# Attention and mixture-of-experts kernel: two loads by halves, three small pieces of work in other slots

## The chip, the cores and the metric

One core of one Trainium2 chip. The metric is the device time of one execution in microseconds (us); lower is better. Engines are named PE (TensorE matmul), DVE (VectorE), ACT (ScalarE), POOL (GpSimd) and SP (SyncE); L789 is line 789 of the kernel. The changed kernel has three more lines near the top, so that L789 of the kernel before is L792 there, L839 is L842, and so on.

## The reference

Attention over keys and values that are averaged in groups of eight, then four dense experts, each weighted by its normalised probability:

```python
# q, k, v: (8 batches, 8 heads, 576 rows, 64); x: (4608, 512); w1: (4, 512, 1024); w2: (4, 1024, 512)
k_p = k.reshape(B, H, 72, 8, D).mean(axis=3)
v_p = v.reshape(B, H, 72, 8, D).mean(axis=3)
attn = softmax(scale * q @ k_p.T)
x = (attn @ v_p)            # back to (B*S, H*D)
p = domain_probs / domain_probs.sum(-1, keepdims=True)
for e in range(4):
    out += p[:, e:e+1] * (relu(x @ w1[e]) @ w2[e])
```

## The kernel before

TensorE is nearly always busy (98% of the span): while the experts of one batch are multiplied, pieces of the attention of the next batches are put into numbered slots between groups of matmuls. Of each batch 512 rows are handled as four token blocks; the 64 rows left over are the "small" ones, handled for two batches together. All loads below are issued by GpSimd, in program order. "Folding" is the averaging over eight rows, done by VectorE in three halving additions.

```python
def load_w2(e):                       # w2 of expert e: 1 MB; only expert 0's comes in halves
    n = 1 if e else 2
    for i in range(n):
        fcs = slice(i * FCH // n, (i + 1) * FCH // n)
        nc.gpsimd.dma_start(out=w2_bf[:, e, fcs], in_=...)

def folds(raw):                       # first two of the three folds
    return [lambda n=n: nc.vector.tensor_add(
        out=raw[:, :, 0:n, :], in0=raw[:, :, 0:n, :], in1=raw[:, :, n:2 * n, :]) for n in (4, 2)]

def context(b, r, c_ps=None):         # 8 matmuls into the bank `att`, then a division by VectorE
    ...
    divide(c_ps, x_tok)

def rem_queries(i):                   # transpose of the small queries, a DMA on SP's queue
    qTr = apool.tile(...)
    nc.sync.dma_start_transpose(out=qTr..., in_=q_rems.pop(i)...)

def rem_scores(i):                    # small scores: 16 matmuls that read qTr
    ...

# first_chunk(), from the third weight sums on (what comes before is cut)
    each(*weight_sums(1)[0:3])
    down_plain(0, 1, 0)               # token block 0 of expert 1; VectorE adds it
    fold_first, *fold_rest = values_folds(1)
    fold_first()
    scores_of_two(1, 2, 0)
    each(*fold_rest)
    load_wide(0, 0); load_q(2); load_wide(0, 1)      # batch 2's keys, queries
    load_wide(1, 0); load_wide(1, 1)                 # batch 2's values
    load_q_rem(0); load_q_rem(1)                     # small queries of batches 0 and 1
    load_wide(1, 2)
    down_plain(0, 1, 1); down_plain(0, 1, 2)
    context(1, 0)
    down_plain(0, 1, 3)
    ...

# slots of batch 2 (BUSY): rem = slots of small queries, scores, context, ...
    plans[BUSY] = dict(
        queries=0, keys=4, values=12, scores=((9, 2), (12, 1), (15, 1)), contexts=(16, 18, 19, 21),
        q=6, k=(5, 8, 11, 14), v=(13, 16, 19, 26), x=(24, 25, 25, 25), rem=(0, 6, 8, 14),
    )
```

The softmax here doesn't subtract the row's maximum and nothing guards it: scores larger than these inputs give would overflow.

Of the kernel before, what the change touches and what calls it, by code (L numbers as in the profile page):

```python
# [17 lines left out]
def kernel(  # L18
# [10 lines left out]
    nc = tc.nc  # L29

    B, H, S, D = q.shape
# [3 lines left out]
    POOL = 8  # L35
# [7 lines left out]
    BUSY = 2  # L43
# [77 lines left out]
        n = 2 if b == 0 else 1  # L121
        return [slice(i * H // n, (i + 1) * H // n) for i in range(n)]

    def load_whole(b, src, nm):

        room = wt_bf[:, 1:E].rearrange("p e s i d -> p (e s i d)")
        at = {"kraw": 0, "vraw": 1}[nm] * H * POOL * D
        raw = room[0:SP, at:at + H * POOL * D].rearrange("j (h r d) -> j h r d", h=H, r=POOL)
        nc.gpsimd.dma_start(out=raw, in_=src[b].rearrange("h (j r) d -> j h r d", r=POOL))
        raws[(nm, b)] = raw  # L130

    def load_first(src, nm, g):
# [60 lines left out]
    def load_q_rem(b):  # L193
        if b % 2 == 0:
            q_rems[b // 2] = qpool.tile([P, H, D], BF16, name="q_rem", bufs=2)
        lo = (b % 2) * REM
        nc.gpsimd.dma_start(
            out=q_rems[b // 2][lo:lo + REM],
            in_=q[b, :, NT:S, :].rearrange("h p d -> p h d"),
        )  # L200
# [10 lines left out]
                )  # L211

    def load_w2(e):
        n = 1 if e else 2
        for i in range(n):
            fcs = slice(i * FCH // n, (i + 1) * FCH // n)
            nc.gpsimd.dma_start(
                out=w2_bf[:, e, fcs], in_=moe_w2[e].rearrange("(fc p) d -> p fc d", p=P)[:, fcs]
            )
# [47 lines left out]



    def folds(raw):  # L270

        return [lambda n=n: nc.vector.tensor_add(
            out=raw[:, :, 0:n, :], in0=raw[:, :, 0:n, :], in1=raw[:, :, n:2 * n, :]) for n in (4, 2)]

    def fold_wide(what, part):
        raw, wide = ((raw_k, wide_k), (raw_v, wide_v))[what]
# [53 lines left out]
        for _ in range(n):  # L330
            nc.tensor.matmul(w_ps[:, 0:cols], lhsT=zeros[:, 0:P], rhs=zeros[:, 0:cols])

    def values_folds(b):
        raw = raw_v if b >= BUSY else raws[("vraw", b)]
        return (folds(raw) if b < BUSY else []) + [lambda: nc.vector.tensor_add(
            out=vps[b % 3][:, :, 0:D], in0=raw[:, :, 0, :], in1=raw[:, :, 1, :])]



# [526 lines left out]
    def first_chunk():  # L866


        def each(*pieces):
            for piece in pieces:  # L870
                piece()

        sums = {e: first_weight_sums(e) for e in range(E)}

        def both(e, step):
            for unit in (1, 0) if e == 3 else (0, 1):
                up_product(0, e, unit, step)

        each(*(lambda n=n: x_sum(0, n) for n in range(4)), *sums[0][0:3])
        norm_probs()  # L880
        up(0, 1, (0, 1))
        hidden_sums(0, 0, 0)
        hidden_sums(0, 0, 1)
        up(0, 1, (2, 3))
        each(*sums[1][0:3])
        up(0, 1, (4,), bank=units[0][1][:])
        each(sums[2][0], sums[2][1], sums[2][3], sums[2][2])
        up(0, 1, (5,), bank=chains[0])
        both(2, 0)
        up(0, 1, (6,), bank=chains[1])  # L890
        both(2, 1)
        up(0, 1, (7,), bank=chains[0])
        last_sum = weight_sums(0)
        each(sums[0][3], sums[1][3], *last_sum[0:2])
        both(2, 2)
        down(0, 0, 0)
        both(2, 3)
        hidden_sums(0, 0, 2)
        down(0, 0, 1)
        both(2, 4)  # L900
        hidden_sums(0, 0, 3)
        down(0, 0, 2)
        both(2, 5)
        each(*last_sum[2:])
        down(0, 0, 3)
        both(2, 6)
        each(*sums[3][0:2])
        both(3, 0)
        down(0, 0, 4)
        both(3, 1)  # L910
        each(sums[3][3], sums[3][2])
        fold_keys(1)
        down(0, 0, 5)
        both(3, 2)
        down(0, 0, 6)
        both(3, 3)
        queries_of_two(0, att[:, 0], nc.scalar.copy)
        both(3, 4)
        both(3, 5)
        keys(1, every)  # L920
        queries_of_two(2, chains[0][:], nc.vector.tensor_copy)
        both(3, 6)
        load_w2(3)
        scores_of_two(1, 0, 0)
        each(*weight_sums(1)[0:3])
        down_plain(0, 1, 0)
        fold_first, *fold_rest = values_folds(1)
        fold_first()
        scores_of_two(1, 2, 0)
        each(*fold_rest)  # L930
        load_wide(0, 0)
        load_q(2)
        load_wide(0, 1)
        load_wide(1, 0)
        load_wide(1, 1)
        load_q_rem(0)
        load_q_rem(1)
        load_wide(1, 2)
        down_plain(0, 1, 1)
        down_plain(0, 1, 2)  # L940
        context(1, 0)
        down_plain(0, 1, 3)
        context(1, 1)
        turn(1, 0)
        hidden_sums(0, 3, 0)
        down_plain(0, 2, 0)
        context(1, 2)
        turn(1, 1)
        hidden_sums(0, 3, 1)
        down_plain(0, 2, 1)  # L950
        context(1, 3)
        turn(1, 2)
        each(*weight_sums(3)[0:3])
        down_plain(0, 2, 2)
        turn(1, 3)
        each(*(lambda n=n: x_sum(1, n) for n in range(3)))

    def pieces_later():


        at, amid = {0: [lambda: x_sum(1, 3)]}, {}

        def put_amid(slot, piece):
            amid[slot] = piece

        def put(slot, *pieces):
            at.setdefault(slot, []).extend(pieces)

        usual = dict(
            queries=-8, keys=-9, values=-2, scores=((2, 2), (9, 2)), contexts=(11, 14, 18, 21),  # L970
            q=1, k=(-2, 0, 5, 9), v=(-2, 0, 5, 9), x=(22, 25, 25, 25), rem=(-3, 17, 24, 25),
        )
        plans = {b: usual for b in range(BUSY, B + 1)}
        plans[BUSY] = dict(
            queries=0, keys=4, values=12, scores=((9, 2), (12, 1), (15, 1)), contexts=(16, 18, 19, 21),
            q=6, k=(5, 8, 11, 14), v=(13, 16, 19, 26), x=(24, 25, 25, 25), rem=(0, 6, 8, 14),
        )
        plans[B] = dict(usual, x=(24, 24, 25, 25), rem=(-3, 17, 21, 22))
        plans[BUSY + 1] = dict(usual, keys=-8, values=4, v=(5, 8, 12, 16))

        for b, plan in plans.items():
            start = 7 * E * (b - BUSY)

            def put_each(what, pieces):
                for slot, piece in zip(plan[what], pieces, strict=True):
                    put(start + slot, piece)

            if b == BUSY:
                put(start + 1, lambda: fold_wide(0, 0))
                put(start + 4, lambda: fold_wide(0, 1))  # L990
                put(start + 5, lambda: load_q_rem(BUSY))
                put(start + 8, lambda: fold_wide(1, 0))
                put(start + 12, lambda: fold_wide(1, 1))
            if b < B:
                put(start + plan["queries"], lambda b=b: queries(b))
                put(start + plan["keys"], lambda b=b: fold_keys(b))
                put(start + plan["keys"] + (b > BUSY), lambda b=b: keys(b, every))
                put(start + plan["values"], *values_folds(b))
                pair = 0
                for slot, n in plan["scores"]:  # L1000
                    if n == 2:
                        put(start + slot, lambda b=b, pair=pair: scores_of_two(b, pair))
                        put_amid(start + slot + 1, lambda b=b, pair=pair: scores(b, pair, 1))
                    else:
                        put(start + slot, lambda b=b, pair=pair: scores(b, pair))
                    pair += n

                for r, slot in zip((2, 3, 0, 1), plan["contexts"]):
                    put(start + slot, lambda b=b, r=r: context(b, r))
                    put(start + slot + 1, lambda b=b, r=r: turn(b, r))  # L1010
            if b + 1 < B:
                put(start + plan["q"], lambda b=b: load_q(b + 1), lambda b=b: load_q_rem(b + 1))
                for what in range(2):
                    put_each("kv"[what], [lambda b=b, what=what, part=part: load_part(b + 1, what, part)
                                          for part in range(NR)])
            if b % 2 == 0:
                i = b // 2 - 1
                put_each("rem", [lambda i=i, do=do: do(i)
                                 for do in (rem_queries, rem_scores, rem_context, rem_turn)])
            put_each("x", [lambda b=b, n=n: x_sum(b, n) for n in range(4)])  # L1020
        return at, amid

    ENG = mybir.EngineType
    with tc.manual_schedule(
# [20 lines left out]
        load_whole(1, k, "kraw")  # L1045
        load_q(1)
        load_w2(1)
        load_whole(1, v, "vraw")
        load_w2(2)
        first_chunk()  # L1050

# [64 lines left out]
```

## Time and profile before

| | kernel before |
|---|---|
| time, 3 runs at hand when the prediction was made | 492.33 us median (491.58 to 493.75) |
| time, 6 runs in the rounds of the comparison | 491.55 us median (491.17 to 493.75) |
| span of the profiled execution | 489.8 us |
| PE / DVE / ACT / POOL busy | 98% / 77% / 62% / 24% |

With TensorE busy for 480.9 of the 489.8 us, only the 8.9 us in which it stands still, the ramp at either end among them, can be won. The prediction shows the lines of the holes that it counts on (A, B, C). Timelines give start us, duration, operation. First, the small scores. The fences below hold three views: SyncE's timeline (start us, duration, operation), the list of DMA issues (KB and us from issue to landing; none given for a transpose), and TensorE's timeline.

```profile
73.56 1.20 SPq L484 DMA_TRANSPOSE qTr<-q_rem  x1
```

```profile
qTr<-q_rem SPq DMA_TRANSPOSE x1, 4.8
```

```profile
78.91 0.41 PE L497 MATMUL att<-qTr,kpT 64*128 64x64 bf16 x16
```

The transposed small queries are issued at 73.56 and land 4.8 us later, near 78.4. TensorE wants them at 78.91. No wait is listed, so it is easy to pass over; but what separates this from a wait is 0.5 us.

Second, the end. VectorE's last addition, then SyncE's waits (us in total, times, longest), then the DMA view from 485.0 to 489.8 us (busy tenths in 40 slices, and the instruction queue q14: packets, MB, share):

```profile
484.60 0.48 DVE L839 SCALAR_TENSOR_TENSOR acc<-o_ps,p_all,acc 128x256 f32<-128x256 f32 x1 [0.39 <-PE o_ps L822]
```

```profile
SPq L1111 <- DMA out_dram<-acc: 2.7, 2, 2.0
```

### The profile page before, as it was taken

The numbers are of one execution on the slowest core, as the hardware profiler recorded it, in microseconds if no ns is written. First come the engines' busy times: TensorE is split into PE (matmuls) and PEld (weight loads), VectorE is DVE, ScalarE is ACT, GpSimd is POOL, SyncE is SP. The second block draws the span as 40 slices with busy tenths as digits, with TensorE's granted clock in tenths as the row PEclk, the third lists the DMA queues.
The fourth block names the chain that finished last, engine by engine and source line by source line (L and its number), as shares of the span: only waits on it lengthen the run. The fifth ranks groups of instructions, "written<-read, shape, count | busy, mean of one in ns | idle before, by whom it ended". The sixth has DMA issues, their size and how long they took to land.

```text
span 489.8 us, 11600 instructions
## 1 busy us (share of the span) xinstructions
PE 480.9 (98%) x4721; PEld 412.2 (84%) x4721; DVE 378.7 (77%) x761; ACT 304.7 (62%) x583; POOL 117.3 (24%) x116
## 2 busy tenths in 40 slices
PE   7999999999999999999999999999999999999995
PEld 4868478888888888888889889888888888888884
DVE  5789999789768976797679876997678766876673
ACT  5787446855676567656765667656755576556650
POOL 8420414242523154016311442111011101110110
PEclk9999999999999999999999999999999999999999
DMA  9999999985997389345955397312111110004003
GB/s 199 210 206 203 192 164 158 103 86 58 116 104 60 79 83 140 34 84 61 154 48 90 28 167 62 70 21 66 34 23 23 38 50 3 12 23 87 0 1 88
DMA packets 101845, 41.98 MB, mean 86 GB/s; under 512 B 73872, under 2 KB 100240, under 8 KB 101792
## 3 DMA queue, kind: packets, MB, share of 16 engines
q0 software_dynamic: 56960, 22.42, 41.0%
q1 hardware_dynamic: 43728, 17.77, 17.0%
q10 hardware_dynamic: 1104, 1.05, 0.6%
q8 instruction: 37, 0.61, 0.5%
q14 instruction: 16, 0.13, 0.1%
HBM read 45.69 MB, written 9.44 MB: 113 GB/s over the span
## 4 chain that ended last, share of the span: by engine, by line
PE 84%; DMA 9%; POOL 2%; DVE 2%; ACT 1%; issue 0%; POOLq 0%; DVEq 0%; ACTq 0%
PE unit L695 39%; PE o_ps L763 39%; DMA w_bf<-in_moe_w_dram 9%; PE o_ps L789 1%; PE att L460 1%; PE unit L822 1%; POOL wt_bf L141 1%; DVE acc L839 1%; PE att L385 1%; POOL w_bf L208 1%; PE unit L385 0%; DVE H L675 0%; PE att L514 0%; DVE x_tok L422 0%; PE att L497 0%
## 5 line engine op out<-in xcount | busy, mean ns | idle before, releaser
L839 DVE SCALAR_TENSOR_TENSOR acc<-o_ps,p_all,acc 128x256 f32<-128x256 f32 (+1 forms) x285 | 127.0, 486 | 51.3 <-PE o_ps L763 36.2
L763 PEld LDWEIGHTS <-H 128*128 128x128 bf16 x1320 | 129.1, 98 | 15.0
L695 PEld LDWEIGHTS <-w_bf 128*128 128x128 bf16 x1088 | 105.2, 98 | 13.0 <-issue 0.2
L675 DVE CUSTOM_DVE_ANT_0 H<-unit,partial 128x512 bf16<-128x512 f32 x128 | 87.4, 685 | 26.1 <-ACT partial L710 12.6
L763 PE MATMUL o_ps<-w_bf,H 128*128 128x256 bf16 x792 | 102.6, 273 | 0.0
L695 PE MATMUL unit<-xT,w_bf 128*128 128x256 bf16 x704 | 100.4, 273 | 0.0
L777 POOL TENSOR_TENSOR acc<-acc,addend 128x512 f32<-128x512 f32 x24 | 30.4, 1266 | 255.5 <-ACT addend L775 211.9
L710 ACT COPY partial<-unit 128x512 f32<-128x512 f32 x128 | 72.3, 592 | 30.0 <-PE unit L695 30.0
L695 PEld LDWEIGHTS <-wu_bf 128*128 128x128 bf16 x816 | 77.6, 98 | 11.7 <-issue 2.5
L695 PE MATMUL unit<-xs,wu_bf 128*128 128x256 bf16 x512 | 77.0, 273 | 0.0
L763 PE MATMUL o_ps<-wt_bf,H 128*128 128x256 bf16 x528 | 68.4, 273 | 0.0
L712 ACT ACTIVATE H<-unit 128x512 bf16<-128x512 f32 x66 | 39.9, 605 | 31.7 <-PE unit L695 31.7
L763 PEld LDWEIGHTS <-S 128*128 128x128 bf16 x528 | 51.7, 98 | 6.0
L716 ACT ACTIVATE H<-unit 128x512 bf16<-128x512 f32 x66 | 39.6, 602 | 26.1 <-PE unit L695 25.8
L708 ACT COPY unit<-unit 128x512 f32<-128x512 f32 x68 | 39.4, 582 | 22.9 <-PE unit L695 17.3
L695 PE MATMUL unit<-xs,w_bf 128*128 128x256 bf16 x256 | 38.4, 273 | 0.0
L837 ACT ACTIVATE acc<-o_ps,p_all 128x256 f32<-128x256 f32 x72 | 30.7, 485 | 9.5 <-PE o_ps L763 7.5
L695 PE MATMUL unit<-xT,wu_bf 128*128 128x256 bf16 x240 | 35.7, 272 | 0.0
L151 POOL DMA_DIRECT2D kraw<-in_k_dram x20 | 26.4, 1320 | 37.6 <-DMA kraw<-in_k_dram 37.6
L763 PE MATMUL o_ps<-wt_bf,S 128*128 128x256 bf16 x264 | 34.2, 273 | 0.0
L763 PE MATMUL o_ps<-w_bf,S 128*128 128x256 bf16 x264 | 34.2, 273 | 0.0
L151 POOL DMA_DIRECT2D vraw<-in_v_dram x20 | 29.0, 1452 | 19.1 <-DMA vraw<-in_v_dram 19.1
(157 smaller groups left out, 506.6 us busy)
## 6 DMA issues: line engine op xcount, KB each, us to landing
out_dram<-acc SPq DMA_DIRECT2D x32, 256.0 KB, 4.5
w_bf<-in_moe_w_dram POOLq DMA_DIRECT2D x6, 1024.0 KB, 18.2
q_sb<-in_q_dram POOLq DMA_DIRECT2D x7, 512.0 KB, 9.9
vraw<-in_v_dram POOLq DMA_DIRECT2D x22, 144.0 KB, 6.8
kraw<-in_k_dram POOLq DMA_DIRECT2D x21, 144.0 KB, 5.8
w_bf<-in_moe_w_dram POOLq DMA_DIRECT2D x3, 512.0 KB, 16.7
wt_bf<-in_k_dram POOLq DMA_DIRECT2D x4, 144.0 KB, 5.4
wt_bf<-in_v_dram POOLq DMA_DIRECT2D x4, 144.0 KB, 4.5
```

The source lines that it names most:

```text
L141: nc.gpsimd.dma_start(out=raw[half * PR:(half + 1) * PR, g].rearrange("j h r d -> j h (r d)"), in_=src[0, h:h + 2].rearrange("h (j r) d -> ...
L151: nc.gpsimd.dma_start(out=raw[:], in_=rows_of(src, b, 2 * part, 2 * part + 2), accum_op=ALU.add if part else ALU.bypass)
L675: nc.vector._custom_dve(TENSOR_ADD_SAT, out=dst, in0=ps, in1=part, s0=LARGEST, s1=0.0)
L695: nc.tensor.matmul(ps[:, n * HN:(n + 1) * HN], lhsT=lhs[:, kc, f:f + P], rhs=rhs[:, kc, :], start=(not grows and n == 0 and kc == 0), stop ...
L708: nc.scalar.copy(out=banks[1][:], in_=ps)
L710: nc.scalar.copy(out=part[:, step - 2], in_=ps)
L712: nc.scalar.activation(out=quarter(0, 0), in_=ps, func=ACT.Relu)
L716: nc.scalar.activation(out=quarter(0, 1), in_=ps, func=ACT.Relu)
L763: nc.tensor.matmul(ps[:, j], lhsT=lhs[:, i, j * P:(j + 1) * P], rhs=rhs[:, i, :], start=(not grows and i == 0 and j == 0), stop=(i == HF - 1),
L777: nc.gpsimd.tensor_add(out=dst, in0=dst, in1=addend[:])
L837: nc.scalar.activation(out=dst, in_=o_ps, func=ACT.Copy, scale=prob)
L839: nc.vector.scalar_tensor_tensor(out=dst, in0=o_ps, scalar=prob, in1=dst, op0=ALU.mult, op1=ALU.add,)
```

## The change

Its intent: let TensorE start on expert 2's w2 when half of it is there; let VectorE hand back a bank between the folds of batch 1's values instead of after them; bring the small queries forward, ahead of batch 2's values, with the small scores a slot later; and move a context so that its bank is free in time.

```diff
-    def load_whole(b, src, nm):
+    def load_whole(b, src, nm, n=1):
...
-        nc.gpsimd.dma_start(out=raw, in_=src[b].rearrange("h (j r) d -> j h r d", r=POOL))
+        for i in range(n):
+            hs = slice(i * H // n, (i + 1) * H // n)
+            nc.gpsimd.dma_start(
+                out=raw[:, hs], in_=src[b].rearrange("h (j r) d -> j h r d", r=POOL)[:, hs])
...
     def load_w2(e):
-        n = 1 if e else 2
+        n = 2 if e in (0, 2) else 1
...   (folds and values_folds take a slice of heads, hs)
-        each(*weight_sums(1)[0:3])
+        rest = weight_sums(1)[0:3]
+        each(*rest[0:2])
         down_plain(0, 1, 0)
-        fold_first, *fold_rest = values_folds(1)
+        lo, hi = slice(0, H // 2), slice(H // 2, H)
+        each(*values_folds(1, lo))
+        scores_of_two(1, 2, 0)
+        fold_first, *fold_rest = values_folds(1, hi)
         fold_first()
-        scores_of_two(1, 2, 0)
+        down_plain(0, 1, 1)
         each(*fold_rest)
         load_wide(0, 0)
         load_q(2)
         load_wide(0, 1)
+        load_q_rem(0)
+        load_q_rem(1)
         load_wide(1, 0)
         load_wide(1, 1)
-        load_q_rem(0)
-        load_q_rem(1)
         load_wide(1, 2)
-        down_plain(0, 1, 1)
         down_plain(0, 1, 2)
         context(1, 0)
+        rest[2]()
...
-            ... contexts=(16, 18, 19, 21),
-            ... rem=(0, 6, 8, 14),
+            ... contexts=(16, 17, 19, 21),
+            ... rem=(0, 7, 8, 14),
...
-        load_whole(1, v, "vraw")
+        load_whole(1, v, "vraw", 2)
```

More of the change, by code (lines that the diff above doesn't have):

```diff
@@ L266, in one_bank, with folds @@
         return spare_bank() if b == 0 else two_banks(b)[:, 0]
-    def folds(raw):
+    def folds(raw, hs=slice(0, H)):
         return [lambda n=n: nc.vector.tensor_add(
-            out=raw[:, :, 0:n, :], in0=raw[:, :, 0:n, :], in1=raw[:, :, n:2 * n, :]) for n in (4, 2)]
+            out=raw[:, hs, 0:n, :], in0=raw[:, hs, 0:n, :], in1=raw[:, hs, n:2 * n, :]) for n in (4, 2)]
     def fold_wide(what, part):
@@ L331, in idle, with values_folds @@
             nc.tensor.matmul(w_ps[:, 0:cols], lhsT=zeros[:, 0:P], rhs=zeros[:, 0:cols])
-    def values_folds(b):
+    def values_folds(b, hs=slice(0, H)):
         raw = raw_v if b >= BUSY else raws[("vraw", b)]
-        return (folds(raw) if b < BUSY else []) + [lambda: nc.vector.tensor_add(
-            out=vps[b % 3][:, :, 0:D], in0=raw[:, :, 0, :], in1=raw[:, :, 1, :])]
+        return (folds(raw, hs) if b < BUSY else []) + [lambda: nc.vector.tensor_add(
+            out=vps[b % 3][:, hs, 0:D], in0=raw[:, hs, 0, :], in1=raw[:, hs, 1, :])]
     def queries(b, pair=0):
@@ L974, in pieces_later @@
         plans[BUSY] = dict(
-            queries=0, keys=4, values=12, scores=((9, 2), (12, 1), (15, 1)), contexts=(16, 18, 19, 21),
-            q=6, k=(5, 8, 11, 14), v=(13, 16, 19, 26), x=(24, 25, 25, 25), rem=(0, 6, 8, 14),
+            queries=0, keys=4, values=12, scores=((9, 2), (12, 1), (15, 1)), contexts=(16, 17, 19, 21),
+            q=6, k=(5, 8, 11, 14), v=(13, 16, 19, 26), x=(24, 25, 25, 25), rem=(0, 7, 8, 14),
         )
```

## The prediction

> **What bounds the kernel now.** I read the page first (busy shares, then the slices), then a table of busy time by stretches, then TensorE's timeline around the one stretch that isn't full, then VectorE's timeline there, and last the chain that ended last.
>
> The page, part 1:
>
> ```profile
> PE 480.9 (98%) x4721; PEld 412.2 (84%) x4721; DVE 378.7 (77%) x761; ACT 304.7 (62%) x583; POOL 117.3 (24%) x116
> ```
>
> TensorE is busy for 480.9 of 489.8 us. Of the 8.9 us that it isn't, 3.1 lie in the first 20 us and 5.2 in the last 9.8 (from the table by stretches: 7.73 and 9.14 of 10 us, and 4.56 of 9.80), which the change doesn't touch. Between 60 and 480 us it is busy everywhere but for 0.07 us near 104. The stretch where the change works has this row (columns: stretch, length, busy us and instructions of each engine, clock, DMA share, GB/s):
>
> ```profile
> 55.00:60.00 5.00, 4.54 (x37) 2.41 (x36) 4.38 (x10) 0.53 (x1) 3.35 (x4) 1.00 1.18 181
> ```
>
> 0.46 us idle, then. TensorE's timeline in it:
>
> ```profile
> 53.09 3.63 PE L789 MATMUL o_ps<-w_bf,H 128*128 128x512 bf16 x16
> 56.55 0.42 PE L460 MATMUL att<-vp,expT 72*128 72x65 bf16 x8
> 57.07 1.89 PE L789 MATMUL o_ps<-w_bf,H 128*128 128x512 bf16 x8
> 58.79 0.42 PE L460 MATMUL att<-vp,expT 72*128 72x65 bf16 x8
> 59.05 0.39 PE L478 MATMUL unit<-ident,x_tok 128*128 128x128 bf16 x4
> 59.80 1.89 PE L789 MATMUL o_ps<-w_bf,partial 128*128 128x512 bf16 x8 [0.36 <-DMA w_bf<-in_moe_w_dram]
> ```
>
> Durations here carry a tail, so I count from start to start. Eight 512-column matmuls take 1.73 us (56.55 - 53.09 = 3.46 for sixteen), eight 65-column ones 0.26 (58.79 to 59.05), four transposes 0.22 (61.79 to 62.01 later on). Two holes appear. The context at 56.55 should give way at 56.81, but the next group starts at 57.07: hole A, 0.26 us, not listed as idle as the tail hides it. The transposes should end at 59.27, but the next group starts at 59.80: hole B, 0.53 us. B is put down to a transfer, and the chain says which:
>
> ```profile
> 28.85 30.91 DMA w_bf<-in_moe_w_dram
> 59.76 0.04 issue
> 59.80 0.38 PE o_ps L789
> ```
>
> It is expert 2's w2, issued at 28.85 and landed whole at 59.76. A is VectorE's; its timeline:
>
> ```profile
> 53.26 0.74 DVE L839 SCALAR_TENSOR_TENSOR acc<-o_ps,p_all,acc 128x512 f32<-128x512 f32 x1
> 53.95 1.95 DVE L272 TENSOR_TENSOR wt_bf<-wt_bf 72x2048 bf16<-72x2048 bf16 x2
> 55.93 0.42 DVE L335 TENSOR_TENSOR vp<-wt_bf 72x512 bf16<-72x512 bf16 x1
> 56.27 1.40 DVE L839 SCALAR_TENSOR_TENSOR acc<-o_ps,p_all,acc 128x512 f32<-128x512 f32 x2
> ```
>
> Token block 3 writes the bank of block 1, whose add stands behind all three folds of batch 1's values. That add runs from 56.27 to about 57.0, just ahead of 57.07.
>
> The third hole, C, is near 104: a context starts at 104.73 where the group ahead (103.62, 0.87 from start to start) ends at 104.49, so 0.24 us.
>
> ```profile
> 103.62 1.04 PE L763 MATMUL o_ps<-w_bf,S 128*128 128x256 bf16 x8
> 104.73 0.42 PE L460 MATMUL att<-vp,expT 72*128 72x65 bf16 x8
> ```
>
> All contexts of a batch share the bank `att`; the next must wait till VectorE has divided the one before (columns as above):
>
> ```profile
> 99.35 0.88 DVE L839 SCALAR_TENSOR_TENSOR acc<-o_ps,p_all,acc 128x256 f32<-128x256 f32 x2 [1.30 <-ACT H L712]
> 100.15 0.20 DVE L421 RECIPROCAL inv<-att 128x8 f32<-128x8 f32 x1
> 100.38 0.69 DVE L422 TENSOR_TENSOR x_tok<-att,inv 128x512 bf16<-128x512 f32 x1
> ...
> 103.98 0.69 DVE L422 TENSOR_TENSOR x_tok<-att,inv 128x512 bf16<-128x512 f32 x1
> ```
>
> The division of the slot 18 context ends at 104.67, which fits 104.73. So A + B + C = 1.03 us, 0.2% of the time, is all that this change can win.
>
> [...] a 512-column matmul is listed with a mean of 379 ns, while starts are 1.73/8 = 216 ns apart; this is what hides A. [...] Here the fold additions take 1218 ns for 2048 elements, 688 for 1024 and 424 for 512: 530 ns per 1024, and about 158 ns left over. [...] an addition of 256 elements should show about 290 ns.
>
> **The change part by part.**
>
> 1. w2 of expert 2 by halves. Expert 0's w2 has already been in halves: the chain has the transfer ahead of it, w1 of expert 2, landed at about 28.6 (13.15 + 15.40), and VectorE waited till 33.72 for the second half of expert 0's w2, which lies just behind. That is 5.1 us for 1024 KB, so 2.6 us a half. The first half of expert 2's should thus land at about 59.8 - 2.6 = 57.2, the second at 59.8 as before. The group that waited can start on its first four matmuls any time after 57.2, and needs the second half 0.87 us after its start: no wait if it starts after 58.9.
>
> 2. Values by halves, and VectorE's order. The new order there is: two weight sums instead of three, add of block 0, three folds of the low heads, first fold of the high heads, add of block 1, the two other folds, add of block 2, division, and only then the third weight sum (0.7 us). From 51.20, with the durations above: sums until 52.6, add 0 from 52.63 (block 0 ends at 52.44 plus its tail) to 53.3; low folds 0.70 + 0.44 + 0.23 until 54.7; high fold until 55.3; add 1 until 56.0; the rest 0.4 + 0.3 until 56.7. Six folds instead of three cost about 0.4 us more in all (2.7 against 2.3), and the values are whole at 56.7 instead of 56.35, so the context starts at about 56.75 instead of 56.55: +0.2. But block 1's bank is free at 56.0, so block 3 follows at once, at 57.0 instead of 57.07. Then block 3 ends at 58.74, context until 59.0, transposes until 59.22, and the waiting group starts at 59.2 instead of 59.80. Its second half is needed at 60.1 and is there at 59.8. Gain of parts 1 and 2: 0.6 us, of 0.79 in A and B.
>
> 3. Small queries of batches 0 and 1 ahead of batch 2's values. Two issues (1.42 us for both) move ahead of two. The batch 2 values are first folded at 82.60 and land near 71.4 (59.21 + 12.2); 1.5 us later is harmless. The transposed small queries wait 0.2 us on SP's queue, off the path. Worth 0 on TensorE. The scores slot moving from 6 to 7 moves sixteen matmuls of 0.34 us by a slot: ACT's exponent stands one copy later, and ACT has 0.84 us idle there. 0.
>
> 4. Context of slot 18 to slot 17. It wins C, as its division then comes before an evacuation and two adds. But at slot 17 the bank must be free too: TensorE gets there at 100.74 (on the clock of before), and the division of slot 16's context ends at 101.07, as the add ahead waited for ACT until 99.35. So 0.24 goes, and about 0.37 comes: net -0.1.
>
> Sum: 0.6 - 0.1 = 0.5 us. From 60 to 104 nothing else stops TensorE, and it runs full to the end, so 0.5 us early here is 0.5 us early at the end: 492.33 - 0.5 = 491.8 us.
>
> **The rivals.** (a) All holes close, also slot 17's, because VectorE, ahead by half a microsecond, divides sooner: 1.0 us, 491.3. For it: the chain from 90 to 104 runs over VectorE and ACT. Against: it starts from a matmul group at 90.17, so it moves as TensorE moves. (b) VectorE takes the gain back. It is busy for 19.08 of 20 us from 60 to 80, and now carries 0.4 us more ahead of that. It would show as a wait of TensorE between 62 and 75: gain 0 to 0.2, 492.2. Against: the first added products need x sums that are ready 1.1 us early (69.0 for 70.08), so there is room for 0.6. (c) The two extra transfers delay the queue. [...] the halves of expert 2's w2 now wait for the halves of expert 0's and are issued near 31 and 34 instead of 28.85. As the queue has some 20 us of work ahead then (the transfer took 30.9 us to land), it shouldn't run dry. If the second half landed 1 us late, B would return: 492.4 or somewhat more.
>
> **Range and chances.** The three runs of before spread over 2.2 us (491.58 to 493.75), four times the gain. The effect itself should lie between -0.4 and +1.0 us; with 0.7 us of scatter in a median I take 490.7 to 492.9. 2% is 9.8 us, ten times what the holes hold, and no transfer is moved by as much: faster 0.005, same 0.985, slower 0.01.
>
> **What would show it.** Right: the 512-column group with the transfer's wait starts near 59.2 and lists no wait on a transfer, block 3 follows its context within 0.3 us of start, first context near 56.75, no TensorE hole at slot 19, and one of 0.3 to 0.4 at slot 17. Wrong: a wait on the transfer still there (part 1), block 1's add still behind the folds (part 2), no hole at slot 17 (part 4, rival a), new TensorE waits between 62 and 75 (rival b), a landing later than 60.1 (rival c).

That a group can start on the first half of a w2 while the second is still on its way (part 1), and that the halves of expert 2's w2 are issued only after those of expert 0's (rival c), are estimates that no trace had shown by then.

## More of the kernel before

```profile
DMA  5998899992039898999941000000000000000000
...
q14 instruction: 1, 0.01, 0.4%
```

The last addition ends at 485.08, and the span 4.72 us after it. In between lie the last two stores, and beside them one fetch of 8 KB of instructions.

## The result, and the profile after

| | before | changed |
|---|---|---|
| time, 6 runs each | 491.55 us (491.17 to 493.75) | 490.01 us (489.34 to 490.66) |
| span of the profiled execution | 489.8 us | 488.7 us |
| VectorE instructions counted | 761 | 764 |

The ratio is 0.996, with a 95% interval from 0.9941 to 0.998: within 2%, as predicted, but the gain is 1.5 us by the medians and not 0.5. 490.01 lies 0.7 us under the range of 490.7 to 492.9.

The holes first. TensorE's timeline around A and B:

```profile
57.18 0.48 PE L463 MATMUL att<-vp,expT 72*128 72x65 bf16 x8
57.50 1.89 PE L792 MATMUL o_ps<-w_bf,H 128*128 128x512 bf16 x8
59.23 0.42 PE L463 MATMUL att<-vp,expT 72*128 72x65 bf16 x8
59.49 0.39 PE L481 MATMUL unit<-ident,x_tok 128*128 128x128 bf16 x4
59.72 1.03 PE L792 MATMUL o_ps<-w_bf,partial 128*128 128x512 bf16 x3
```

From start to start: 0.32, 1.73, 0.26 and 0.23 us. Block 3 follows its context (A is closed) and the group that waited for w2 lists no wait (B is closed). The halves of that w2, issued at 31.42 and 33.96 (GpSimd waited 1.80 and 1.76 us before them, for transfers of `w_bf`), landed 24.4 and 24.5 us later, at 55.8 and 58.5: 2.7 us apart, where 2.6 were predicted. Yet the group starts at 59.72 and not at 59.2, for TensorE is late here from something new, the only wait on its list between 20 and 480 us:

```profile
PE o_ps L792 <- DMA w_bf<-in_moe_w_dram: 0.6, 1, 0.6
```

That is w2 of expert 1, which landed late in this execution. And around slots 17 and 19:

```profile
99.78 1.04 PE L766 MATMUL o_ps<-wt_bf,S 128*128 128x256 bf16 x8
100.67 0.42 PE L463 MATMUL att<-vp,expT 72*128 72x65 bf16 x8
...
103.55 1.04 PE L766 MATMUL o_ps<-w_bf,S 128*128 128x256 bf16 x8
104.42 0.42 PE L463 MATMUL att<-vp,expT 72*128 72x65 bf16 x8
```

Both contexts start when the group ahead is through (0.89 and 0.87 us after its start): C is closed, and the hole predicted at slot 17 isn't there. VectorE shows why: the addition ahead of that division came sooner than it did before, where it waited 1.30 us for another releaser (the line is in the prediction):

```profile
98.91 0.88 DVE L842 SCALAR_TENSOR_TENSOR acc<-o_ps,p_all,acc 128x256 f32<-128x256 f32 x2 [0.93 <-ACT partial L713]
```

So at 104.42 TensorE is 0.31 us ahead of before (104.73), and still is at the end: VectorE's last addition starts 0.30 us sooner. But the span is 1.1 us shorter. The other 0.8 us comes after the last addition:

```profile
484.30 0.48 DVE L842 SCALAR_TENSOR_TENSOR acc<-o_ps,p_all,acc 128x256 f32<-128x256 f32 x1 [0.39 <-PE o_ps L825]
```

```profile
SPq L1118 <- DMA out_dram<-acc: 1.9, 2, 1.2
```

The addition ends at 484.78 and the span 3.92 us later (4.72 before); the longest wait for a store is 1.2 us instead of 2.0. The DMA view of this stretch has no line for q14: the fetch came at 482.7, some 2 us before the addition ended and ahead of the last stores.

And the small queries. Views as before:

```profile
72.45 1.19 SPq L487 DMA_TRANSPOSE qTr<-q_rem  x1
```

```profile
qTr<-q_rem SPq DMA_TRANSPOSE x1, 2.5
```

```profile
80.58 0.41 PE L500 MATMUL att<-qTr,kpT 64*128 64x64 bf16 x16
```

They land near 75.0, 5.6 us ahead of their use; before it was 0.5.

Two things were thus open: what the 0.8 us at the end come from, which no part of the change was meant to touch, and how one pair of traces with 0.3 us of TensorE gain fits a difference of 1.5 us in the medians.

### The profile page after: what moved, and what is told of

Same layout as the page of the kernel before. It is cut to its first block, busy times and chain, and to the rows that moved or that the text cites. A ratio compares the mean times of both kernels' runs of the same rounds, so it can differ in the third digit from the quotient of the medians. Undisturbed runs are those within 1.5% of the kernel's fastest.

```text
span 488.7 us, 11602 instructions
## 1 busy us (share of the span) xinstructions
PE 480.9 (98%) x4717; PEld 412.2 (84%) x4721; DVE 378.9 (78%) x764; ACT 304.8 (62%) x583; POOL 118.4 (24%) x118
## 4 chain that ended last, share of the span: by engine, by line
PE 89%; DMA 8%; POOL 2%; issue 0%; DVE 0%; POOLq 0%
PE unit L698 40%; PE o_ps L766 40%; DMA w_bf<-in_moe_w_dram 8%; PE o_ps L792 3%; PE att L463 2%; PE unit L825 1%; POOL wt_bf L144 1%; PE att L388 1%; PE unit L388 1%; POOL w_bf L211 0%; PE att L517 0%; PE att L500 0%; PE unit L481 0%; POOL q_sb L181 0%; PE o_ps L825 0%
## 6 DMA issues: line engine op xcount, KB each, us to landing
w_bf<-in_moe_w_dram POOLq DMA_DIRECT2D x5, 1024.0 KB, 15.6
```

## The experiments

All kernels were correct, and all were timed in five rounds. Runs of one group are from the same chip. The label's first two characters name the group; the kernel before had a median of 491.85 (c1), 491.92 (c2), 492.25 (c3) and 492.42 us (c4).

| run | median us (range) | ratio, 95% interval |
|---|---|---|
| c1_same_before | 493.17 (491.72 to 494.13) | 1.0009 (0.9971 to 1.0046) |
| c1_same_after | 489.78 (489.55 to 490.15) | 0.9944 (0.9909 to 0.9978) |
| c1_only_w2 | 493.47 (491.17 to 497.0) | 1.0022 (0.9972 to 1.0071) |
| c1_only_values | 490.05 (489.66 to 491.02) | 0.995 (0.9915 to 0.9985) |
| c2_pad_before | 491.13 (490.45 to 494.17) | 0.9991 (0.9968 to 1.0014) |
| c2_only_small | 491.03 (490.86 to 491.65) | 0.9984 (0.997 to 0.9998) |
| c2_only_contexts | 492.17 (491.45 to 492.88) | 1.0002 (0.9987 to 1.0017) |
| c2_w2_of_1_too | 489.81 (489.62 to 490.42) | 0.9958 (0.9944 to 0.9971) |
| c3_pad_early | 491.02 (490.49 to 492.19) | 0.9972 (0.9946 to 0.9999) |
| c3_contexts_pad_early | 491.36 (490.99 to 493.87) | 0.9983 (0.9953 to 1.0012) |
| c3_small_pad_early | 490.19 (489.99 to 490.85) | 0.9954 (0.9928 to 0.998) |
| c3_undo_contexts | 489.75 (489.46 to 490.19) | 0.9944 (0.9915 to 0.9972) |
| c4_after_less3 | 491.03 (490.73 to 491.75) | 0.997 (0.9954 to 0.9985) |
| c4_same_after | 490.18 (489.9 to 491.58) | 0.9957 (0.994 to 0.9973) |

**The two kernels again.** No edit.

> The kernel before, unchanged, against itself. Both theories: ratio 1.000 within 0.2%; this is the noise of a comparison. Theory L (landing): hole B, in front of the 512-column group that waits for expert 2's w2, is set by when that transfer lands, so in this second trace it has another size than 0.53 us, by several tenths, while hole A (0.26 us) and hole C (0.24 us) are as before. Rival V (VectorE's order): all three holes repeat within 0.05 us.

> The changed kernel, unchanged. Ratio 0.996 to 0.998. Theory L: the wait of 0.61 us for expert 1's w2 (third-last token group of expert 1's first block) is a matter of that transfer's landing and will differ by several tenths in this second trace; without it the kernel gains about 1 us (A, B and C). Rival V: the wait repeats as it belongs to the new order. [...] the time from the last VectorE add's end to the end of the span differs between kernels in the same sense again (before 4.7 us, changed 3.9); if it is scatter, it doesn't.

The difference is 2.07 us between the changed kernel and the kernel before of the same rounds (491.85), if anything more than at first. But the kernel before, run against itself, had medians of 493.17 and 491.85 in these rounds, 1.3 us apart: a single difference of less than that shows little by itself, and the traces must carry the argument. In the second trace of the changed kernel the wait for expert 1's w2 is gone, and the ends are again 4.7 and 3.9 us long. And the second trace of the kernel before is not the first one over. Hole A is there (0.20 us) and C (0.23), but B is not: w2 of expert 2 had landed. In its place TensorE stands still where the first trace had no wait. SyncE's timeline, the landing, and TensorE:

```profile
74.36 1.19 SPq L484 DMA_TRANSPOSE qTr<-q_rem  x1
```

```profile
qTr<-q_rem SPq DMA_TRANSPOSE x1, 5.3
```

```profile
79.73 0.41 PE L497 MATMUL att<-qTr,kpT 64*128 64x64 bf16 x16 [1.32 <-DMA qTr<-q_rem]
```

The transposed small queries were issued 0.8 us later than in the first trace and took 0.5 us longer. I call this wait hole D. Part 3 of the change bears on it: it issues the small queries sooner and uses them later.

**One part at a time.**

```diff
 # c1_only_w2
-        n = 1 if e else 2
+        n = 2 if e in (0, 2) else 1
```

> Kernel before with only expert 2's w2 in halves. Theory L: the wait on the transfer is gone, the group starts right behind the transposes, hole A (0.26) and C (0.24) stay: 0.5 us or more gained, ratio 0.998 to 0.999. Rival V: less than 0.3 us, ratio 0.9995.

No gain shows (ratio 1.0022, with an interval that reaches from 0.9972 to 1.0071). B is not there, but its trace has D (0.90 us), a wait of 0.34 us for expert 1's w2, C, and a wait of 1.16 us for VectorE at 121.42 that no other trace has and that stays unexplained.

c1_only_values is the changed kernel with w2, the small queries' order and slot, and the context put back.

> Kernel before with only batch 1's values in halves and VectorE's new order. Theory L: hole A goes but the group still waits until the whole of expert 2's w2 has landed, so the gain is 0 to 0.2 us, ratio 1.000. Rival V: this part carries the gain, 0.8 us or more, ratio 0.998.

This has nearly all of the gain: 490.05. So Theory L missed twice (it gave w2 alone 0.5 us or more, and values alone at most 0.2), and rival V had the times right, though not for the reason it gave. The trace has neither A nor B nor C nor D. B and D say little here, as TensorE was 1.2 us later than in the first trace from the start of this stretch on (51.40 against 50.17), after waits at 15.6 and 17.4 us. That C is gone can't come from its bank, as the context is back at slot 18; and the span ends 3.93 us after the last addition. Both pointed to something that values in halves bring along. One such thing is plain: the halves cost VectorE three folds more, so it has three more instructions.

```diff
 # c2_only_small
+        load_q_rem(0)
+        load_q_rem(1)
         load_wide(1, 0)
         load_wide(1, 1)
-        load_q_rem(0)
-        load_q_rem(1)
-            ... rem=(0, 6, 8, 14),
+            ... rem=(0, 7, 8, 14),
```

> Kernel before, with only the small queries of batches 0 and 1 ahead of batch 2's values and the small scores at slot 7. Theory D (a fourth hole): two of four traces without this part show TensorE waiting 1.3 and 0.9 us at the small scores for the transposed small queries; here they come 1.4 us sooner and are wanted 1.7 us later, so no such wait in the trace, and the runs scatter less upwards (none beyond 493). Holes A, B, C and the 4.7 us end stay. Median 0 to 1 us below before. Rival (my prediction): worth nothing, same median and same scatter as before.

0.9 us under the kernel before by the medians (the interval reaches from 0.1 to 1.5 us), and its runs lie within 0.8 us. TensorE lists no wait between 20 and 480 us: D is gone. A (0.20) and C (0.23) stay, and the end is 4.65 us. So part 3, to which I gave 0, is worth more by the medians than all that I had summed. Its two halves were not run apart: the transposes landed near 77.0 here, which would have been in time for the old slot too (near 78.0).

```diff
 # c2_only_contexts
-            ... contexts=(16, 18, 19, 21),
+            ... contexts=(16, 17, 19, 21),
```

> Kernel before, with only the context of slot 18 at slot 17. My prediction: hole C (0.24 us) goes and one of about 0.37 us appears at slot 17, net -0.1. Rival (as both traces of the changed kernel suggest): no hole at slot 17 and none at slot 19, 0.24 us gained. In the times neither is clear of the scatter; the trace decides. Small-scores wait of 0 to 1.3 us as in before.

No gain (1.0002). Here the hole at slot 17 is just as predicted. TensorE, then VectorE:

```profile
100.77 1.04 PE L763 MATMUL o_ps<-wt_bf,S 128*128 128x256 bf16 x8
102.02 0.42 PE L460 MATMUL att<-vp,expT 72*128 72x65 bf16 x8 [0.22 <-DVE x_tok L422]
```

```profile
100.26 0.88 DVE L839 SCALAR_TENSOR_TENSOR acc<-o_ps,p_all,acc 128x256 f32<-128x256 f32 x2 [1.30 <-ACT H L712]
```

The context was due at 100.77 + 0.87 = 101.64 and starts at 102.02: 0.38 us. The addition ahead of the division waits 1.30 us, as in the kernel before. C is gone, as predicted. The trace also has D (0.81 us) and a wait of 0.37 us for ScalarE at 70.98.

**The end of the kernel.** Theory F: neither w2 nor the values matter to the end. What matters is the number of VectorE's instructions, which sets when a fetch of 8 KB of instructions comes (queue q14 moved 16 of that size in each trace of the pair, the last at 486.9 us before and at 482.7 us changed). The first test adds three tiny instructions to the kernel before, late in it, and nothing else:

```diff
 # c2_pad_before
+    pad = const.tile([P, 8], BF16, name="pad")
             if g == 7 * (N - 2):
                 load_last_weights()
+                for _ in range(3):
+                    nc.vector.memset(pad[:], 0.0)
```

> Kernel before, plus three 8-column memsets of VectorE on a tile nobody reads, late in the kernel; nothing else. Theory F (fetch): the kernels with values in halves end 0.8 us sooner after their last VectorE add because their three more VectorE instructions move the last instruction fetch of 8 KB from beside the last stores to some 4 us ahead of them. Then the same happens here: last add's end to span's end 3.9 us instead of 4.7, the last fetch ahead of the last add, time 0.8 us lower (ratio 0.998). Rival S: the shorter end belongs to the new order or to chance; then 4.7 us as before and ratio 1.000.

VectorE's end and SyncE's waits:

```profile
483.98 0.48 DVE L840 SCALAR_TENSOR_TENSOR acc<-o_ps,p_all,acc 128x256 f32<-128x256 f32 x1 [0.39 <-PE o_ps L823]
```

```profile
SPq L1114 <- DMA out_dram<-acc: 1.9, 2, 1.2
```

The end is 488.4 - 484.46 = 3.94 us, with the same 1.9 and 1.2 us as in the changed kernel, and the fetch fell at 482.4. The median fell by 0.8 us; the interval of the ratio still includes 1, as one run took 494.17, but the lowest time fell too (490.45 against 491.11). With more work in it, the kernel ends sooner after its last addition. C stayed in it (0.23 us at slot 19), as the memsets come after that.

```diff
 # c2_w2_of_1_too, from the changed kernel
-        n = 2 if e in (0, 2) else 1
+        n = 2 if e < 3 else 1
```

> The changed kernel with expert 1's w2 in halves too, as a version that might beat it: one of two traces of the changed kernel waited 0.61 us for the whole of that transfer. If landing is what matters: no wait there, ratio to before a little below the changed kernel's 0.994 to 0.996 (0 to 0.6 us). Rival: the wait is rare[...]: same or slower.

489.81, no better than the changed kernel in other rounds: no sign that waits for w2 decide.

**Slot 17 and hole C.** If the count of instructions sets when they are fetched, the same could hold for the addition near 99 us. Now the three memsets stand at the start of the kernel, so that a fetch near 99 us can move as well.

```diff
 # c3_pad_early
+    pad = const.tile([P, 8], BF16, name="pad")
+    for _ in range(3):
+        nc.vector.memset(pad[:], 0.0)
 # c3_contexts_pad_early: the same, and contexts=(16, 17, 19, 21)
 # c3_small_pad_early: the same, and the edit of c2_only_small
 # c3_undo_contexts: the changed kernel with contexts=(16, 18, 19, 21)
```

> The kernel before with three 8-column memsets on VectorE at the start, where VectorE waits for data anyway; nothing else. Theory F (where VectorE's instruction fetches fall depends on how many instructions went before, and a fetch beside the last stores costs 0.8 us; another near 99 us holds VectorE's add for 0.36 us): last add to end of span 3.9 us instead of 4.7, the add near 99.3 released 0.93 us after idle begins rather than 1.30, hole C (0.24 us at slot 19) gone, median 0.8 to 1.1 us under before. Rival G (the add near 99 comes earlier because the values are in halves): end at 3.9 us, but the add still waits 1.30 us and hole C is there; 0.6 to 0.8 us under before. Rival H (only late memsets did it by chance): same as before.

> Context of slot 18 at slot 17 plus the three early memsets. Theory F: the hole of 0.38 us that slot 17 had with this part alone closes (add ahead released 0.36 us earlier), end of span 3.9 us after the last add: 0.8 to 1.2 us under before. Rival G: the hole of 0.38 us at slot 17 stays; 0.3 to 0.7 us under before.

> Small queries ahead of batch 2's values (and small scores at slot 7) plus the three early memsets; no w2 or values in halves, no context moved. If the changed kernel's gain is mostly the end of the kernel (0.8 us) and the transposed small queries (0 to 1.3 us), this has nearly all of it: 490.0 to 490.4, tight over runs. If the halves of values and w2 carry it: 490.8 to 491.2.

> The changed kernel with the context back at slot 18. If part 4 is worth nothing in the full change (hole C closes also without it, as with values alone): the changed kernel's 489.8 to 490.0, no hole at slot 19. If part 4 is what closes hole C: 0.24 us more, 490.0 to 490.3, hole of 0.24 us at slot 19.

VectorE and TensorE with the early memsets alone:

```profile
100.34 0.88 DVE L842 SCALAR_TENSOR_TENSOR acc<-o_ps,p_all,acc 128x256 f32<-128x256 f32 x2 [0.93 <-ACT partial L713]
```

```profile
102.96 1.04 PE L766 MATMUL o_ps<-wt_bf,H 128*128 128x256 bf16 x8
103.84 0.42 PE L463 MATMUL att<-vp,expT 72*128 72x65 bf16 x8
```

The addition waits 0.93 us instead of 1.30, and hole C is closed: the context starts 0.88 us after the group ahead of it. And with the context moved as well (c3_contexts_pad_early), the hole at slot 17 closes too:

```profile
100.54 1.04 PE L766 MATMUL o_ps<-wt_bf,S 128*128 128x256 bf16 x8
101.43 0.42 PE L463 MATMUL att<-vp,expT 72*128 72x65 bf16 x8
```

So rival G (values in halves do it) falls. c3_pad_early's time was 1.2 us under the kernel before, somewhat more than the expected 0.8 to 1.1. Its own trace shows the worst D of all, 1.73 us. The small queries with the memsets, and no other part, take 490.19; all of the change but the context takes 489.75. In these rounds the medians make a ladder:

| step | time us | span us | time less span |
|---|---|---|---|
| kernel before | 492.25 | 490.2 | 2.04 |
| three more VectorE instructions | 491.02 | 489.0 | 2.01 |
| and part 3 (small queries ahead) | 490.19 | 488.15 | 2.06 |
| parts 1, 2, 3, the three extra instructions being folds | 489.75 | 488.05 | 1.73 |

Part 4, the context, is worth nothing on top: without it the changed kernel is as fast as with it in other rounds (489.75 against 489.78 and 490.18), and there is no hole at slot 19. Parts 1 and 2 take off 0.1 us of the span here, which is within the scatter (487.9 to 488.8 and 487.7 to 488.5), and 0.3 us of the time outside the span.

**Taking three instructions away.** The last test goes the other way. The changed kernel fills the ones column of its value tiles with three small memsets on VectorE; these go to GpSimd, so that VectorE has as many instructions as in the kernel before.

```diff
 # c4_after_less3
     for vp in vps:
-        nc.vector.memset(vp[:, :, D:D + 1], float(POOL))
+        nc.gpsimd.memset(vp[:, :, D:D + 1], float(POOL))
```

> The changed kernel with its three small memsets of the ones column moved from VectorE to GpSimd, so that VectorE has as many instructions as in the kernel before; the four parts are all there. Theory F (instruction fetches): the end of the span comes 4.7 us after the last add again, the add near 99 us waits 1.30 us again, and a hole of about 0.37 us at slot 17 appears as predicted on paper: 0.8 to 1.3 us over the changed kernel, 490.6 to 491.1. Rival (the end of 3.9 us and the earlier add come from the change's parts themselves): 489.8 to 490.0 as the changed kernel.

> The changed kernel again, as the neighbour of the one above on the same chip: 489.6 to 490.1 whichever theory holds.

VectorE, TensorE, SyncE's waits, and the instruction queue between 485.0 and 489.2 us:

```profile
98.63 0.88 DVE L842 SCALAR_TENSOR_TENSOR acc<-o_ps,p_all,acc 128x256 f32<-128x256 f32 x2 [1.30 <-ACT H L715]
```

```profile
99.14 1.04 PE L766 MATMUL o_ps<-wt_bf,S 128*128 128x256 bf16 x8
100.40 0.42 PE L463 MATMUL att<-vp,expT 72*128 72x65 bf16 x8 [0.22 <-DVE x_tok L425]
```

```profile
SPq L1118 <- DMA out_dram<-acc: 2.6, 2, 2.0
```

```profile
q14 instruction: 1, 0.01, 0.7%
```

All three come back. The addition waits 1.30 us, the predicted hole at slot 17 opens (due at 99.14 + 0.87 = 100.01, so 0.39 us), the end takes 489.2 - 484.50 = 4.70 us, and a fetch lies at 486.2. The kernel is 0.85 us slower than its neighbour (491.03 against 490.18). That is near the lower end of the expected 0.8 to 1.3 us, and the median stands inside 490.6 to 491.1.

## Why the prediction was wrong

**"Worth 0 on TensorE" (part 3) failed.** I read "wait 0.2 us on SP's queue, off the path" and did not ask how far the landing was from its reader. It was 0.5 us in the trace at hand; the other traces without part 3 and without values in halves had waits of 1.32, 0.90, 0.81, 1.73, 0.17 and once none (0.2 us of margin, c2_pad_before). Alone the part won 0.9 us, and 0.83 us on top of the memsets. That D was absent from c1_only_values is no doing of its halves: GpSimd issued the small queries at 60.45 there (60.51 in c1_same_before), they landed near 79.1 as elsewhere, and TensorE, itself late, came for them at 79.43. From issue to landing the same transpose took from 4.6 us (c2_pad_before) to 6.2 us (c3_pad_early) in kernels without part 3, and 2.4 us (c1_same_after) to 3.9 us (c2_only_small) in kernels with it. That spread and the time of issue made hole D.

**"5.2 in the last 9.8, which the change doesn't touch" failed.** The end shrank by 0.8 us. That three VectorE instructions do it is shown in both directions: added to the kernel before they take 4.7 to 3.9 us, taken from the changed kernel they bring 4.7 back. All 16 traces agree: the six with 761 instructions end 4.66 to 4.71 us after the last addition, the ten with 764 end 3.92 to 3.95 us after it. In the six a fetch of 8 KB starts 1.7 to 1.8 us after the addition's end, amid the packets of the last two stores; in the ten it started 2 us before the addition's end. The packets show what it meets. The last store that ScalarE's queue (q10) issues has 144 packets. In the ten all have started by 2.5 us after the addition. In the six, 9 of them start only 2.8 us after it, behind the fetch and the rest of SyncE's last store (through at 2.15 us in the ten, at 2.8 us in the six). In the trace of the kernel before, these 9 are what is left of q10 (packets, MB, share) from 487.75 us on:

```profile
q10 hardware_dynamic: 9, 0.01, 1.1%
```

In the changed kernel no packet of any queue lies in the same stretch after its last addition (487.45 us on). So the fetch goes with a delay of these 9 packets and of SyncE's last ones. That the fetch itself causes it is the likely reading; it was moved only by way of the count.

**Part 4's arithmetic was right for the wrong kernel.** With the context moved, the hole at slot 17 came as worked out (0.37 predicted; 0.38 and 0.39 measured) in both traces in which VectorE had the old number of instructions up to there, and in none of the five in which it had three more. I took the 1.30 us wait of the addition for a dependence on ACT. But it had its data: the matmul group ahead of it started 1.49 us earlier (97.86 to 99.35), where 1.13 us were enough in the changed kernel (97.78 to 98.91). These 0.36 us go with the number of instructions ahead of it: 1.30 us of wait in seven traces, 0.93 or 0.94 in the nine others. In each of the seven a fetch of 8 KB starts 0.65 to 0.69 us after the addition does (at 100.0 in the kernel before, 99.3 in c4_after_less3); in the nine there is none between 98 and 102 us. The addition can't have waited for a fetch that starts after it: what holds it is not resolved.

**Rival (a) was nearest, and for another reason.** It had all holes closed and 491.3. It named VectorE's lead of half a microsecond as the cause. There was no such lead: in the profiled pair TensorE was just 0.08 us ahead at the w2 group (59.72 against 59.80).

**Parts 1 and 2 did what was said, for less.** A closed and B closed. But A held 0.20 or 0.21 us in six other traces instead of 0.26 (0.37 in c2_only_contexts), and B exists only when w2 lands late: 0.53 us in the trace that I read, and none in any of the eight other traces with w2 whole. I took one execution's landing time for a property of the kernel. In the ladder, parts 1 and 2 hold 0.1 us of the span instead of 0.6. A wait that I had not counted may belong to part 1: three of the six traces with only expert 2's w2 newly in halves wait 0.34 to 0.61 us for expert 1's, and none of the nine with both whole. Whether the halves bring it was not tested.

**"492.33 - 0.5".** The base was a median of three; six runs gave 491.55. Beyond that, kernels with values or w2 in halves spend 1.7 to 1.9 us outside the span instead of 2.05, whatever their span (medians of five or six runs: 1.75 changed, 1.71 values only, 1.74 w2 only, 1.86 with expert 1's w2 too, 1.87 with three instructions less; 2.03 same before, 2.06 small queries only). For the changed kernel that is 0.3 us of the gain. These kernels have more transfers on GpSimd's queue, but the one with the most has 1.86, and why the time outside the span is shorter stays open.

**The sum, redone.** In group c1 the gain was 2.07 us: 0.8 at the end, 0.3 outside the span, and about 1.0 left for TensorE. For that there are A at 0.2, C at 0.24 and D, whose share is not settled: the small queries had 0.83 us in the ladder, but c1_only_values, without them, has 1.80 of the 2.07 us. Of the predicted terms only A held, about a tenth of the gain. C closed too, but through the number of VectorE's instructions, with part 4 or without it.

None of the versions beats the changed kernel by more than its scatter. The two nearest, without the context's move (489.75) and with expert 1's w2 in halves too (489.81), tie with it.

## What to carry to other kernels

A transfer that lands 0.5 us before its reader is a wait that this one trace happens not to show: list the margin of each landing beside the waits, and expect the landing to vary between executions (here from 78.1 to 80.2 us, over seven traces without part 3 and without values in halves). Before a difference under a microsecond is put down to a change's intent, add and take away as many idle instructions on the engine concerned as the change does, at the start of the kernel (here three such instructions went with 1.2 us, c3_pad_early). And a single trace's hole that ends with a DMA is a sample (hole B: 0.53 us in one trace, none in the eight other traces with w2 whole); look at a second execution before giving it a size.
